# Transposing most of the normalized tokens by DMA in a fused attention and gated-MLP kernel on one Trainium2 core

## The chip, the cores and the metric

The kernel runs on one core of a Trainium2 chip. The core has a matrix engine (PE, TensorE), a vector engine (DVE, VectorE), a scalar engine for activation functions (ACT, ScalarE), a general engine (POOL, GpSimd) and a sync engine (SP) whose queue issues the DMAs here. SBUF is the on-chip working memory of 128 partitions; PSUM holds matmul results in 8 banks. Each engine works through its own instructions in order and waits on semaphores for the others. The metric is the device time of one execution in microseconds (us); lower is better.

## The reference, cut to what matters

```python
x = A_x                              # (1, 2048, 1024), bf16
xn = layernorm(x)                    # no scale, no bias
s = attention(xn)                    # 32 heads of 32: qkv = xn @ wqkv; softmax(q k^T / sqrt(32)) v; @ wo
y = layernorm(xn)
h = gelu(y @ w1 + b1)                # 1024 -> 3584, tanh form
g = silu(h @ w2 + b2)                # 3584 -> 1024
return x + s * g
```

Attention is over all 2048 tokens without a mask. Its 32 x 2048 x 2048 exponentials are the largest amount of elementwise work.

## The kernel before, in words

**Layout.** The 2048 tokens are 16 tiles of 128. Matmuls need the normalized tokens with the model dimension on the partitions, so each tile is normalized token-wise (`xnb`, four buffers used in turn) and transposed into `xnT`, a tensor of 128 partitions x 8 chunks x 2048 tokens. The second layernorm needs no new transpose: `make_y` scales `xnT` by one number per token.

**First stage.** DMAs on SP's queue load the x tiles (line 728), and, between them, the weights for the keys and queries of head group 0 and for the values (lines 739, 744). VectorE takes statistics of each tile (869, 871) and, for a pair of tiles, prepares variance and mean (884, 886). POOL raises the variance to the power -0.5 (888), forms the product with the mean (890) and normalizes each tile into its `xnb` buffer (898); tiles 0 and 1 are normalized by VectorE (879). Then `tr_item` transposes a tile: eight PE transposes against the identity into one PSUM bank (849), and one ScalarE copy of 128x1024 into `xnT` (860; half of tile 1 is copied by VectorE, 858). When both tiles of a pair are there, PE projects their keys (`k_pair_item`, copied out at 814) and, two pairs later in the list, their values (`v_item`, copied out at 786).

**Attention.** Four heads form a head group, and there are eight groups. Work goes by units: group, block of 256 queries, pair of 128-key tiles; 64 units a group, 512 in all. A unit is eight score matmuls on PE (1125), two exponentials on ScalarE of 128x1024 each (1134), and eight PV matmuls (709). The sums of the exponentials over the keys come from VectorE, which adds tiles in three levels (1155, 1160, 1163), and from matmuls with ones; a level that would come late is left out, and PE adds the unsummed tiles instead. `norm` divides (1199 to 1211). Units run in order of their keys, so unit number 7, the last of the first query block, needs the keys of tiles 14 and 15.

**MLP and output.** The MLP runs over chunks of 256 tokens beside the attention, with w1 in a ring of three buffers (936) and w2 in a ring of four (942). Its result goes to DRAM (1041). In the last head group the output projection (`wo`, queue "wo") runs for each query block: four items of eight matmuls, an evacuation that multiplies by the gate (1301), an addition of x (1308, or 1305 on POOL), and a store (1312, 1316). For the last block, matmuls 0 to 6 of an item and matmul 7, which alone needs the last head group, are separate pieces of the order that share a PSUM bank (`host`, `wob`).

**What sets the order.** `_Plan` holds every operation with an assumed duration, its reads and writes and a priority. `run` lays them out on the five engines ahead of time by these assumed durations: scores first on PE, then PV and key sums, then the "dense" queues `pro`, `proj`, `mlp`, `wo`, the last in the order in which items were added. `settle` turns the dependences into semaphore waits, and `emit` writes each engine's instructions in that fixed order. So a changed operation changes the order on every engine, down to the last unit.

Of the kernel before, what the change touches and what calls it, by code (L numbers as in the profile page):

```python
# [40 lines left out]
EVD = ()  # L41
ENGS = ("PE", "ACT", "DVE", "POOL", "SP")
# [7 lines left out]
class _Item:  # L50
    def __init__(self, kind, due=0):
        self.kind = kind
        self.due = due
        self.after = 0
        self.need = []
        self.last = False
        self.host = None
        self.chunks = []
        self.evacs = []
        self.bank = None  # L60
        self.k = 0


class _Plan:
# [3 lines left out]
    def __init__(self):  # L68
# [5 lines left out]
        self.wob = []  # L74
# [39 lines left out]
    def run(self, total_units, dense_slack):  # L114
# [28 lines left out]
        def commit(o, t):  # L143
            e = o.eng
            o.start = t
            if e == "SP":
# [7 lines left out]
                o.fin = state["bw"] + 1900.0  # L154
# [107 lines left out]
        def pe_step(t):  # L262
# [40 lines left out]
            for it in self.wob:  # L303
                if it.k == 0 and it.host.k == len(it.host.chunks) and it.chunks[0].left == 0:
                    cands.append((it.chunks[0].ready, 1.5, it.chunks[0], (it, it.host.bank, None)))
                    break
# [81 lines left out]
            if cls == 1.5:  # L388
                opening[0].bank = opening[1]
            elif opening is not None:  # L390
# [19 lines left out]
            else:  # L410
                it = o.item
                it.k += 1
                if it.k == len(it.chunks):
                    if cls == 1:
                        state["pvopen"] = None
                    elif cls == 1.5:
                        state["done"] += o.occ
# [126 lines left out]
def bass_recurrent_scan__mha_block__mixer_channel_mlp__prompt_kernel(  # L544
# [38 lines left out]
    with ExitStack() as st:  # L583
# [143 lines left out]
        def load_x(t):  # L727
            dma(f"x{t}", lambda e: e.dma_start(xst[t], x2[t * 128:(t + 1) * 128, :]), 262144, [], [XS(t)] + al_x_w(t))

        def al_x_w(t):  # L730
            return []
# [3 lines left out]
        def load_qk(hg, which):  # L735
# [3 lines left out]
            dma(f"wqk{i}", lambda e: e.dma_start(wqk[i], src), 262144 * 3 // 2, [], [("wqk", i)])  # L739
# [13 lines left out]
        for t in range(6, NT):  # L753
            load_x(t)
# [109 lines left out]
        XV = lambda t: ("xst", t)  # L864
        pro_q.append(warm_item())
        for n in range(NPR):
            for t in (2 * n, 2 * n + 1):
                for c in range(2):
# [3 lines left out]
                    150, [("st", t, 0), ("st", t, 1)], [("mv", t)], 1)  # L872
            lo, hi = 2 * n, 2 * n + 2
# [18 lines left out]
            for t in (lo, lo + 1):  # L892
# [5 lines left out]
                pool(lambda e, t=t: e.tensor_scalar(xnb[t % 4], xst[t], lnp[:, t, 1:2], lnp[:, t, 5:6],  # L898
                                                    op0=ALU.mult, op1=ALU.add), 950,
                     [XS(t), ("nb_", n), ("rs", n)], [("xnb", t % 4)], 1)  # L900
            pro_q += [tr_item(lo), tr_item(lo + 1), k_pair_item(n, False)]
# [30 lines left out]
        def load_w1(p):  # L932
# [3 lines left out]
            dma(f"w1{gi}", lambda e: e.dma_start(w1r[gi][:], src), 524288, [], [("w1", gi)])  # L936
# [213 lines left out]
        def ones_four(u, pv):  # L1150
# [15 lines left out]
            def o_fn(e, b):  # L1166
# [13 lines left out]
                return ins  # L1180
            oc = add("PE", lambda e: o_fn(e, pv.bank), Q256, TL,
# [6 lines left out]
            last = HG * 64  # L1188
            for op, more, off in ((add2[0], 2, u < NOPA), (add2[1], 2, u < NOPA or u + 4 >= last),
                                  (add4[0], 1, u < NOPA), (add4[1], 1, u < NOPA or u + 4 >= last),  # L1190
                                  (add8, 1, u < NOPA or u + 4 >= last)):
                if off:
                    plan.skip.append(op)
                    oc.occ += more * Q256
            return oc
# [18 lines left out]
        OTr = xnT  # L1214
        for tq in range(1, 4):
            plan.queues["proj"].append(qk_item(0, 0, tq, wq0, 16 * tq - 12))
            plan.queues["proj"][-1].after = 1000
        for w in range(HG):
# [23 lines left out]
            for qb in range(NQB):  # L1242
# [4 lines left out]
                for kp in range(NKP):  # L1247
# [3 lines left out]
                    if kp % 4 == 3:  # L1251
                        ocs.append(ones_four(g * 8 + kp - 3, pv))
                pv.chunks = [vcs[0:6] + ocs[0:1] + vcs[6:8] + ocs[1:2], vcs + ocs][OLAG]
# [9 lines left out]

                for t2 in range(2):
                    tb = 2 * qb + t2
                    ri = tb % 4
                    if ri < 2:
                        xr = V[:, ri].rearrange("p t n -> p (t n)")[:, 0:1024]
                        gr = V[:, ri].rearrange("p t n -> p (t n)")[:, 1024:2048]
                        rt = [("V", ri, n) for n in range(NPR)]  # L1270
                    elif ri == 2:
                        yf = yT[:].rearrange("p c t -> p (c t)")
                        xr, gr = yf[:, 0:1024], yf[:, 1024:2048]
# [105 lines left out]
```

## Time and profile before

| | us |
|---|---|
| median of three runs (lowest, highest) | 1063.63 (1062.75, 1064.71) |
| the profiled execution | 1063.63 |
| its span in the profile | 1061.6 |
| busy in the span: PE, ScalarE, VectorE, POOL | 1025.0, 1024.8, 972.6, 34.1 |
| granted PE clock, mean | 0.997 |

A group row of the profile names the line of the code, the engine, the operation, the tile written and the tiles read, shapes and count; then the busy time in us and the mean duration of one in ns; then the engine's idle time just before them and what ended most of it. A timeline row gives the start in us, the duration, the engine, line and operation, and in brackets the idle time before it and its releaser. A row of DMA issues ends with the size of one and the median time from issue to landing. Instructions that follow one another on an engine overlap by some tens of ns, so the durations of neighbours can add to slightly more than the stretch they fill. A busy PE is not PE at its peak, since matmuls are pipelined and their ends are modelled.

### The profile page before, as it was taken

To read this page: it belongs to the slowest core of one execution; us is meant where nothing else is said; L and a number is where in the kernel's file an instruction comes from. 1 tells how busy PE (TensorE), PEld (TensorE's weight loads), DVE (VectorE), ACT (ScalarE), POOL (GpSimd) and SP (SyncE) were. 2 spreads that over 40 slices of the span, in tenths; PEclk is the share of its full clock that TensorE was granted. 3 is DMA by queue.
4 is the path that set the end of the run, shared out by engine and by line. 5 is a ranking of instruction groups with operands and counts; after the bars stand their busy time and mean duration, and the time that the engine had idled before them with its cause. 6 is when DMAs were issued, how large, how long until landed. Compare 5 with 4: busy or idle time off the path is not lost.

```text
span 1061.6 us, 32119 instructions
## 1 busy us (share of the span) xinstructions
PE 1025.0 (97%) x14334; PEld 637.7 (60%) x14334; DVE 972.6 (92%) x1506; ACT 1024.8 (97%) x1114; POOL 34.1 (3%) x42
## 2 busy tenths in 40 slices
PE   7898999999999999999999999999999999999998
PEld 5655466646666556656666556656665566665443
DVE  8899999998899999898899989999999899978896
ACT  5899999999999999999999999999999999999994
POOL 5600000000000000000000000000000000000000
PEclk9999999999999999999999999999999999999999
DMA  9334257723276436723365546533566577673442
GB/s 268 91 104 132 58 163 198 212 84 86 76 214 187 114 108 198 202 75 105 104 194 164 144 120 188 166 86 95 143 194 173 160 228 218 195 204 92 140 130 81
DMA packets 285796, 156.49 MB, mean 147 GB/s; under 512 B 23642, under 2 KB 276570, under 8 KB 285658
## 3 DMA queue, kind: packets, MB, share of 16 engines
q1 hardware_dynamic: 285658, 154.44, 50.9%
q8 instruction: 112, 1.84, 0.7%
q14 instruction: 26, 0.21, 0.1%
HBM read 142.35 MB, written 12.06 MB: 145 GB/s over the span
## 4 chain that ended last, share of the span: by engine, by line
PE 48%; ACT 43%; DMA 4%; DVE 3%; POOL 1%; issue 0%; POOLq 0%
ACT P L1134 40%; PE ps L714 32%; PE ps L1125 8%; PE ps L709 8%; DMA w1r<-in_B_w_dram 3%; ACT ut L1000 3%; DVE ut L869 1%; DMA w2r<-in_B_w_dram 1%; POOL gw L898 0%; POOL lnp L912 0%; DMA hT<-in_A_x_dram 0%; DVE xb L985 0%; DVE PA L1155 0%; DVE lnp L884 0%; ACT gw L1036 0%
## 5 line engine op out<-in xcount | busy, mean ns | idle before, releaser
L1134 ACT ACTIVATE P<-ps 128x1024 bf16<-128x1024 f32 x1024 | 960.7, 1189 | 10.2 <-PE ps L1125 9.8
L1155 DVE TENSOR_TENSOR PA<-P 128x2048 bf16<-128x2048 bf16 x251 | 303.9, 1212 | 16.6 <-ACT P L1134 15.4
L714 PE MATMUL ps<-yT,w1r 128*128 128x256 bf16 x1792 | 233.2, 274 | 7.1 <-DMA w1r<-in_B_w_dram 4.4
L714 PE MATMUL ps<-w2r,hT 128*128 128x256 bf16 x1792 | 228.6, 274 | 1.5 <-DVE hT L1003 0.6
L714 PEld LDWEIGHTS ps<-yT,w1r 128*128 128x128 bf16 x1792 | 163.1, 98 | 65.8 <-issue 32.7
L714 PEld LDWEIGHTS ps<-w2r,hT 128*128 128x128 bf16 x1792 | 162.0, 98 | 54.9 <-issue 33.4
L709 PE MATMUL ps<-P,V 128*32 128x256 bf16 x4096 | 146.3, 276 | 1.1 <-ACT P L1134 0.5
L1160 DVE TENSOR_TENSOR PA<-PA 128x1024 bf16<-128x1024 bf16 x202 | 137.8, 689 | 1.7
L714 PE MATMUL ps<-big,qk 128*128 128x512 bf16 (+2 forms) x568 | 130.6, 360 | 2.6 <-DVE V L786 0.8
L714 PE MATMUL ps<-qk,big 128*128 128x256 bf16 (+1 forms) x736 | 124.8, 306 | 0.4 <-DVE V L1301 0.2
L709 PEld LDWEIGHTS ps<-P,V 128*32 128x32 bf16 x4096 | 97.7, 97 | 34.9 <-issue 22.4
L1125 PE MATMUL ps<-qk 32*128 32x256 bf16 x2048 | 102.1, 274 | 9.1 <-ACT P L1134 6.8
L1125 PE MATMUL ps<-QKT 32*128 32x256 bf16 x2048 | 101.7, 273 | 5.0 <-ACT P L1134 4.8
L714 PEld LDWEIGHTS ps<-qk,big 128*128 128x128 bf16 x736 | 65.5, 98 | 39.6 <-issue 15.2
L985 DVE TENSOR_TENSOR xb<-ps,b1T 128x512 bf16<-128x512 f32 x112 | 76.8, 686 | 11.4 <-PE ps L714 10.2
L714 PEld LDWEIGHTS ps<-big,qk 128*128 128x128 bf16 x568 | 47.7, 98 | 54.2 <-issue 15.0
L1003 DVE SCALAR_TENSOR_TENSOR hT<-ut,xb 128x512 bf16<-128x512 f32 x112 | 74.1, 680 | 2.2 <-ACT ut L1000 2.0
L1125 PEld LDWEIGHTS ps<-QKT 32*128 32x128 bf16 x2048 | 30.3, 92 | 72.4 <-ACT P L1134 68.1
L1125 PEld LDWEIGHTS ps<-qk 32*128 32x128 bf16 x2048 | 30.4, 92 | 72.1 <-ACT P L1134 62.4
L998 DVE SCALAR_TENSOR_TENSOR ut<-hT,xb 128x1024 f32<-128x1024 bf16 x56 | 68.2, 1220 | 0.1
L1000 ACT ACTIVATE ut<-ut 128x1024 f32<-128x1024 f32 x56 | 67.3, 1207 | 0.0
L1199 DVE STREAM_TRANSPOSE nt<-ps 128x256 f32<-128x256 f32 x64 | 28.7, 449 | 27.5 <-PE ps L709 27.1
(76 smaller groups left out, 568.5 us busy)
## 6 DMA issues: line engine op xcount, KB each, us to landing
w1r<-in_B_w_dram SPq DMA_DIRECT2D x112, 512.0 KB, 4.6
w2r<-in_B_w_dram SPq DMA_DIRECT2D x128, 448.0 KB, 4.4
qk<-in_A_wqkv_dram SPq DMA_DIRECT2D x16, 256.0 KB, 3.4
g_scratch<-gw SPq DMA_DIRECT2D x32, 128.0 KB, 4.2
o_scratch<-ot SPq DMA_DIRECT2D x56, 64.0 KB, 3.2
big<-o_scratch SPq DMA_DIRECT2D x28, 128.0 KB, 3.7
hT<-in_A_x_dram SPq DMA_DIRECT2D x10, 256.0 KB, 4.5
qk<-in_A_wqkv_dram SPq DMA_DIRECT2D x4, 512.0 KB, 3.8
```

Source lines behind the costliest of these rows:

```text
L709: ins = e.matmul(dst(j), lhsT=lhsT(j), rhs=rhs(j), start=start, stop=stop, tile_position=(0, 32 * j), skip_group_check=True)
L714: return e.matmul(dst, lhsT=lhsT, rhs=rhs, start=start, stop=stop, skip_group_check=True)
L869: dve(lambda e, t=t, c=c: e.bn_stats(stats[:, t, c, :], xst[t][:, c * 512:(c + 1) * 512]), 600, [XS(t)], [("st", t, c)], 1)
L985: dve(lambda e: e.tensor_tensor(xb_t[i2][:, p % 2].rearrange("p (k t) -> p k t", k=2), bank(it.bank).rearrange("p (k t) -> p k t", k=2), b ...
L998: dve(lambda e, r=r: e.scalar_tensor_tensor(ut_t[i2][:, r], h[:, r], 1.0 / GA, xb[:, r], op0=ALU.add, op1=ALU.mult), c_f32(r.stop - r.star ...
L1000: act(lambda e: e.activation(ut_t[i2][:], ut_t[i2][:], ACT.Tanh, scale=GC * GA), c_acts(1024), [("ut", i2, 0), ("ut", i2, 1)], [("ut", i2, ...
L1003: dve(lambda e, r=r: e.scalar_tensor_tensor(h[:, r], ut_t[i2][:, r], 1.0, xb[:, r], op0=ALU.add, op1=ALU.mult), c_f32(r.stop - r.start), [ ...
L1125: ins = e.matmul(bank(b0[j], kk * 256, (kk + 1) * 256), lhsT=QKT[sl][32 * j:32 * j + 32, 1, kb * 128:(kb + 1) * 128], rhs=QKT[sl][32 * j:3 ...
L1134: x = act(lambda e, h=h: e.activation(P[pi][:, 2 * h:2 * h + 2].rearrange("p j k q -> p (j k q)"), ps[:, pr[h] * 1024:(pr[h] + 1) * 1024], ...
L1155: add2.append(dve(lambda e, p0=p0, a0=a0: e.tensor_tensor(PA_all[:, a0:a0 + 2].rearrange("p u j q -> p (u j) q"), P_all[:, p0:p0 + 2, :, 0 ...
L1160: add4.append(dve(lambda e, a0=a0: e.tensor_tensor(PA[a0], PA[a0], PA[a0 + 1], op=ALU.add), c_b16(1024), [("PA", a0 + 1)], [("PA", a0)], P ...
L1199: a = dve(lambda e: e.transpose(nt_t[i][:], bank(pv.bank, 256, 512)), c_ps(256), [], [("nt", i)], 1, pv)
```

## The change

Tiles 0 and 1 are transposed as before. For tiles 2 to 15 the PE transposes and the ScalarE copies are replaced by one DMA each, issued on SP's queue, which reads the `xnb` buffer and writes the tile's columns of `xnT` transposed. A buffer can be overwritten when that DMA has landed. Loads around it are moved: x tile k, for k from 8 on, is not issued before the statistics of tile k - 8 have begun; the third load of key or query weights waits until tile 15 is normalized; the first three w1 loads wait until tiles 9, 11 and 13 are normalized.

The end is changed too. The output projection of the last query block is split in another way: for its four items matmuls 0 to 6 are separate items, added to the queue behind block 5 (`PART`), evacuated to float32 partial sums in SBUF that already contain the gate and x; the last items have one matmul each, an evacuation with the gate and an addition of the partial sum. Their x and gate tiles are in two w1 buffers of their own (numbers 4 and 5). In the last group of four units the key sums' second half is left to PE in two pieces.

```diff
+PART = 5
+TD = 2
+XA = 8
+XB = 8
+XW = 9
...
-                o.fin = state["bw"] + 1900.0
+                o.fin = state["bw"] + (2600.0 if o.sem.startswith("tp") else 1900.0)
...
-        for t in range(6, NT):
+        for t in range(6, XA):
             load_x(t)
...
+                for k in range(XA, NT):
+                    if max(0, k - XB) == t:
+                        load_x(k, [("st", t, 0)])
...
-            pro_q += [tr_item(lo), tr_item(lo + 1), k_pair_item(n, False)]
+            for t in (lo, lo + 1):
+                if t < TD:
+                    pro_q.append(tr_item(t))
+                else:
+
+                    add("SP", lambda e, t=t: e.dma_start_transpose(out=xnT[:, :, t * 128:(t + 1) * 128], in_=xnb[t % 4]),
+                        1500, 0, [("xnb", t % 4)], [("xnT", t, h) for h in range(2)], 0, sem=f"tp{t % 4}", nbytes=360000)
+            pro_q.append(k_pair_item(n, False))
...
-            dma(f"w1{gi}", lambda e: e.dma_start(w1r[gi][:], src), 524288, [], [("w1", gi)])
+            dma(f"w1{gi}", lambda e: e.dma_start(w1r[gi][:], src), 524288, [], [("w1", gi)], 3,
+                [xnop[XW + 2 * p]] if p < 3 else [])
...
+            if hi < HG:
+                dve(lambda e: e.scalar_tensor_tensor(pk, bank(it.bank), 0.5, gr[:, sl], op0=ALU.mult, op1=ALU.mult),
+                    c_ps(512), g, pt, 0, it)
+                dve(lambda e: e.tensor_tensor(pk, pk, xr[:, sl], op=ALU.add), c_f32(512), x + pt, pt, 2.4)
+            else:
+                dve(lambda e: e.scalar_tensor_tensor(gr[:, sl], bank(it.bank), 0.5, gr[:, sl], op0=ALU.mult, op1=ALU.mult),
+                    c_ps(512), g, g, 0, it)
+                if lo == 0:
+                    dve(lambda e: e.tensor_tensor(xr[:, sl], gr[:, sl], xr[:, sl], op=ALU.add), c_b16(512), g + x, x, 1)
+                else:
+                    last = lambda e: e.tensor_tensor(xr[:, sl], gr[:, sl], pk, op=ALU.add)
+                    if t2 == 0:
+                        pool(last, 1100, g + pt, x, 1)
+                    else:
+                        dve(last, c_f32(512), g + pt, x, 1)
...
                 for t2 in range(2):
...
+                    if not lastq:
+                        wo_load(qb, t2)
                     for nh in range(2):
...
+                        wo_item(qb, t2, nh, 7 if lastq else 0, 8)
...
+                if qb == PART:
+
+                    for t2 in range(2):
+                        wo_load(NQB - 1, t2)
+                        for nh in range(2):
+                            wo_item(NQB - 1, t2, nh, 0, 7)
```

## The prediction, made before the changed kernel was run

> **What bounds the kernel now.** I read the busy times first, then stages, then the hand-over between the first stage and the long middle, then the end. In the table of stages each engine's busy time is followed by its number of instructions; the cuts are at the first exponential of the unbroken run (46.0 us) and at the end of the last one (1047.0 us).
>
> ```profile
> PE 1025.0 (97%) x14334; PEld 637.7 (60%) x14334; DVE 972.6 (92%) x1506; ACT 1024.8 (97%) x1114; POOL 34.1 (3%) x42
> ```
> ```profile
> 0.00:46.00 46.00, 36.66 (x398) 26.24 (x399) 39.88 (x96) 29.70 (x33) 31.80 (x40) 1.00 0.68 199
> 46.00:1047.00 1001.00, 977.19 (x13864) 606.38 (x13862) 924.46 (x1395) 995.12 (x1082) 0.00 (x0) 1.00 0.51 146
> 1047.00:1061.60 14.60, 11.15 (x76) 5.07 (x74) 8.25 (x16) 0.00 (x0) 2.31 (x2) 1.00 0.20 72
> ```
> The columns after the length are PE, its weight loads, VectorE, ScalarE and POOL. ScalarE is busy 995.1 of 1001.0 us in the middle: the middle is its exponentials and tanh calls end to end, with 5.9 us of gaps. So the time is three pieces in a row: when the unbroken run starts (46.0), its length (1001), and what follows its last exponential (14.6). In the first stage ScalarE idles 16.3 us, so work taken from it there is worth nothing unless the run starts earlier.
>
> What the removed work costs, from the groups of instructions by shape:
> ```profile
> L1134 ACT ACTIVATE P<-ps 128x1024 bf16<-128x1024 f32 x1024 | 960.7, 1189 | 10.2 <-PE ps L1125 9.8
> L860 ACT ACTIVATE big<-ps 128x1024 bf16<-128x1024 bf16 x15 | 15.1, 1026 | 11.2 <-PE ps L849 11.2
> L849 PE MATMUL ps<-ident,gw 128*128 128x128 bf16 x96 | 7.2, 220 | 3.8 <-DVE gw L879 2.2 <-POOL gw L898 1.6
> ```
> What starts the run, from the timelines of POOL and ScalarE:
> ```profile
> 33.88 1.73 POOL L888 TENSOR_TENSOR lnp<-lnp,mhalf 128x2 f32<-128x2 f32 x1
> 35.69 0.89 POOL L890 TENSOR_TENSOR lnp<-lnp 128x2 f32<-128x2 f32 x1
> 37.20 1.20 POOL L898 TENSOR_SCALAR gw<-w2r,lnp 128x1024 bf16<-128x1024 bf16 x1
> 38.38 1.62 POOL L898 TENSOR_SCALAR yT<-w2r,lnp 128x1024 bf16<-128x1024 bf16 x1
> ```
> ```profile
> 41.83 1.02 ACT L860 ACTIVATE big<-ps 128x1024 bf16<-128x1024 bf16 x1 [0.78 <-PE ps L849]
> 42.75 1.94 ACT L1134 ACTIVATE P<-ps 128x1024 bf16<-128x1024 f32 x2
> 45.98 1.94 ACT L1134 ACTIVATE P<-ps 128x1024 bf16<-128x1024 f32 x2 [1.29 <-PE ps L1125]
> ```
> POOL normalizes one tile after another and ends tile 15 at 40.00. Its transpose, copy, key projection and scores follow, and the first exponential that needs those keys starts at 45.98, which is 5.98 us later. Before it only 14 exponentials (seven units) can run, whatever ScalarE has free. POOL, busy 9.2 and 9.6 of 10 us in 20 to 40 us, and the last tile's path set the start.
>
> The end, from PE's and VectorE's timelines, and the landing times of the DMA issues:
> ```profile
> 1047.17 0.40 PE L709 MATMUL ps<-P,V 128*32 128x256 bf16 x8
> 1048.05 1.25 PE L714 MATMUL ps<-qk,big 128*128 128x512 bf16 x5
> ```
> ```profile
> 1058.19 0.69 DVE L1301 SCALAR_TENSOR_TENSOR w1r<-ps,w1r 128x512 bf16<-128x512 f32 x1 [0.57 <-PE ps L714]
> 1058.92 0.42 DVE L1308 TENSOR_TENSOR w1r<-w1r 128x512 bf16<-128x512 bf16 x1
> ```
> ```profile
> qk<-in_A_wqkv_dram SPq DMA_DIRECT2D x16, 256.0 KB, 3.4
> hT<-in_A_x_dram SPq DMA_DIRECT2D x10, 256.0 KB, 4.5
> w2r<-in_A_x_dram SPq DMA_DIRECT2D x6, 256.0 KB, 6.4
> out_dram<-V SPq DMA_DIRECT2D x8, 256.0 KB, 2.0
> ```
> After the last PV matmuls 46 matmuls of the output projection remain, one per 0.2175 us (five take 1.09). VectorE ends at 1059.34, and 2.26 us later the last store has landed.
>
> **The change, part by part.** The profiled execution took 1063.63 us, the median of the runs; its span is 1061.6, so 2.0 us lie around it.
>
> *Removed in the first stage.* 14 ScalarE copies at 1.026 = 14.4 us, and 14 times 8 PE transposes at some 0.62 = 8.7 us. PE's own share shrinks the backlog in the middle, where PE already waits for ScalarE; ScalarE's share only widens its 16.3 us of idle time. Worth by themselves: 0.
>
> *The transposes' path.* From a normalized tile to its exponential the path was 5.98 us. Now: a DMA of landing time L, then the key projection 1.05, VectorE's copy 0.42, scores to exponential 0.45, and some 0.2 for hand-overs: L + 2.1. The trace has no transposing DMA and none from SBUF to SBUF. Bounds for L are its 256 KB rows: 2.0 (stores) and 6.4 (x tiles behind others). The nearest is the 256 KB load in 256-byte runs, the length that the transposes write, 3.4; since it moves data without turning it, I take 4.5, the next row up. Path 6.6, so +0.6 us (-1.9 to +2.5).
>
> *POOL's new waits.* Each normalized tile sits in one of four buffers. PE freed it at once; now the tile four later waits until the DMA has landed. The built order also puts the power for tiles 8 and 9 ahead of normalizing tiles 6 and 7, so these wait for VectorE's statistics, at some 22.2 us (23.10 before, less a key and a value copy, 1.1, that stand later now, plus a 0.16 copy). Carried through at 1.20 a tile, 0.90 a pair's power and product, with VectorE's statistics at 25.2, 29.4 and 32.4 (3.0 a pair: four at 0.64 and three small steps; 4.2 where a key and a value copy stand between): tiles 6 and 7 end at 25.4 (23.2 before), 11 at 32.7, 13 at 36.0, and, with three small steps (1.6) put in between, tile 15 at 40.0. At L = 4.5 the buffers are free in time; at 6.4 they add 1.2. Before, the last pair lost 1.03 + 0.70 + 0.42 = 2.15 us to stretched steps (1.73, 0.89 and 1.62 against 0.70, 0.19 and 1.20), while VectorE ran its first key sums; those run beside POOL again. I take half: tile 15 at 41.0, +1.0 (-0 to +3.3).
>
> *SP's queue.* 14 transposes are issued ahead of the first w1 and w2 loads. If an issue took 1.84 us, the crowded w1 issue (three in 5.53), 14 would take 25.8, within POOL's 27. x tiles 8 to 15 now wait for statistics of the tile eight before; the last lands at about 22, its statistics come after 29. The weights are issued from some 42 us, three w1 and four w2 at up to 1.84: done by 57, first used near 57: 0, and up to +2 if the cover is gone. The waiting instruction on SP has only those loads behind it.
>
> *The middle.* The same 1010 exponentials and 72 tanh calls run after the start. VectorE gets 3 sums of 1.21, 7 less 1 of 0.69, and four partial results at 0.69 + 0.69: +13.3 us on an engine at 92%. PE loses 8.7 and 1.3 (48 key-sum matmuls at 0.0275). The gaps of 5.9 may shrink or grow: 0 (-4 to +4).
>
> *The end.* The partial sums for the last two token tiles stand in the built order before the previous block's output projection, and are late themselves: 12 of their 28 matmuls stand behind the last PV. After it there are 48 matmuls now, 46 before. First matmul at +0.73 us from the last exponential (+1.06 before; 12 key-sum matmuls fewer), last one through at +11.2, as before. Then it was one evacuation, one add, one store: +14.6. Now the four final matmuls come in a row, so VectorE has a value evacuation until +11.2, four evacuations at 0.64 until +13.8, a 0.42 add, two adds with a float32 operand at 0.65 (0.42 for half the columns, L1211): +15.5. With 2.26 for the store: +17.8. That is +3.2 (+2 to +4).
>
> Sum: 0.6 + 1.0 + 0 + 3.2 = +4.8 us: 1068.4.
>
> A rule of the Trainium skill stands against the change: VectorE: DVE Perf Modes, section "The three transpose paths", gives a 128x128 transpose 390 ns on TensorE and 1309 ns by DMA. This trace shows eight PE transposes in 0.62 us, less than the page says, and no DMA transposes. An estimate by that page, eight blocks one after another, is 10.5 us a tile and 147 us for 14: the kernel would end about 110 us later. DMA: Bandwidth & Descriptors, "Latency and other measured facts", has 261 GB/s for a DMA transpose, by which (an estimate) a tile moves in 1.0 us and my sum holds.
>
> **Rivals.** *Slow transposes.* Above L of some 5 the ring of four buffers paces POOL: each us of L costs about 2.5 us (1.0 on the last path, 1.5 in the ring). L = 8 gives +8.6 at the start and, with the end, 1075; L = 12 about 1085. For: no row excludes it. Against: all 256 KB rows lie under 6.4.
>
> *Nothing to tell.* L near 3 and VectorE's sums clear of POOL: start -1, gaps -1, end +3.2: 1064.8; with the gaps gone 1061.5. For: PE's load falls. Against: the end is plain in the built order.
>
> *Faster.* The removed ScalarE time comes off the start: ScalarE is 9.87 of 10 us busy in 20 to 30 us, and if that, not POOL, paces the first stage, up to 14.4 us go: 1052. It decides once the unbroken run starts before 46.0 - 3.2 - 2.1 = 40.7. Against: tile 15 was normalized only at 40.0, and POOL had gaps of 0.1.
>
> **How the numbers follow.** A change under 0.2% (2.1 us) is about what this kernel's measurement can't tell from none. Forecast (1066 to 1073) 0.56; slow transposes 0.15; nothing to tell 0.15; faster 0.14. Slower is 0.71. All lower bounds at once (-1.9, 0, -4, +2) give 1059.7, all upper ones (+2.5, +3.3, +2, +4, +4) 1079.4. I go from 1061 to 1077, which leaves out some 0.1 of the faster case below and 0.1 of the slow transposes above.
>
> **What would show it.** Right: 14 exponentials before the run, the run's start at 46.5 to 49, transposes landing in 3.5 to 6 us, ScalarE over 99% busy until its last exponential, and 17 to 18 us after it. Wrong: a start before 44 (POOL was held by others), POOL waiting on the transposes for microseconds a tile, ScalarE gaps in the middle beyond 10 us, or an end of 15 us or less.

## The result, and the profile after

The changed kernel took 1072.01 us (median of four runs, 1070.72 to 1073.35) beside 1064.17 for the kernel before: 1.0075 times as long, 95% interval 1.0057 to 1.0094. On another chip it took 1069.66 beside 1063.57, 1.0052 (1.0033 to 1.0071). By these ratios it is slower by 5.5 to 8.0 us; 4.8 had been forecast. Its profiled execution took 1072.81 us with a span of 1071.0.

The stages of the changed kernel, cut at the first exponential of the unbroken run and at the end of the last one, as before (PE, weight loads, VectorE, ScalarE, POOL, clock, DMA share, GB/s):
```profile
0.00:51.67 51.67, 37.58 (x301) 25.55 (x302) 41.74 (x98) 16.57 (x18) 31.97 (x40) 0.87 0.84 190
51.67:1052.82 1001.15, 975.58 (x13810) 603.11 (x13808) 928.06 (x1402) 994.71 (x1082) 0.00 (x0) 1.00 0.53 149
1052.82:1071.00 18.18, 11.38 (x66) 4.95 (x64) 13.64 (x24) 0.00 (x1) 2.28 (x2) 0.91 0.16 58
```
The middle is what it was (1001.15 against 1001.0). The start is 5.7 us later and the end 3.6 us longer. ScalarE lost 13 us of work in the first stage, and its idle time there grew from 16.3 to 35.1 us.

**The start.** POOL's timeline in the changed kernel: the power for tiles 8 and 9, which stands ahead of normalizing tiles 6 and 7; the power for the last pair; and the normalizations of tiles 12, 14 and 15:
```profile
23.62 0.70 POOL L884 TENSOR_TENSOR lnp<-lnp,mhalf 128x2 f32<-128x2 f32 x1 [1.67 <-DVE lnp L882]
...
35.05 0.70 POOL L884 TENSOR_TENSOR lnp<-lnp,mhalf 128x2 f32<-128x2 f32 x1 [1.23 <-DVE lnp L882]
35.73 2.27 POOL L894 TENSOR_SCALAR gw<-w2r,lnp 128x1024 bf16<-128x1024 bf16 x1
...
39.95 2.24 POOL L894 TENSOR_SCALAR gw<-w2r,lnp 128x1024 bf16<-128x1024 bf16 x1
...
43.16 1.19 POOL L894 TENSOR_SCALAR yT<-w2r,lnp 128x1024 bf16<-128x1024 bf16 x1
```
Tile 15 is normalized at 44.35, 4.35 us later than before. POOL waited for VectorE, never for a transpose, and two normalizations took 2.27 and 2.24 us instead of 1.19.

TensorE's timeline in the same kernel, and three windows of 2 us with its granted clock (the third number from the right):
```profile
19.98 1.89 PE L709 MATMUL ps<-qk,big 128*128 128x256 bf16 x8 [3.84 <-DMA big<-gw]
...
28.06 0.61 PE L1129 MATMUL ps<-qk 32*128 32x256 bf16 x8 [3.78 <-DVE qk L807]
28.61 2.10 PE L709 MATMUL ps<-qk,big 128*128 128x256 bf16 x9
30.50 1.91 PE L709 MATMUL ps<-big,qk 128*128 128x256 bf16 x8
```
```profile
10.00:12.00 2.00, 2.00 (x21) 2.00 (x20) 1.60 (x5) 0.12 (x1) 0.00 (x0) 0.50 1.09 338
20.00:22.00 2.00, 2.00 (x10) 1.44 (x11) 2.00 (x5) 0.00 (x0) 1.76 (x3) 0.50 1.15 241
28.00:30.00 2.00, 1.94 (x15) 1.16 (x16) 2.00 (x6) 1.27 (x2) 2.00 (x3) 0.50 0.70 132
```
PE waited 3.84 us for the first transposed tile, and 3.78 us for VectorE's copy of the second pair's keys (L807), which stands behind statistics in VectorE's order. After each wait its clock was granted at half, and eight key matmuls took 1.91 us; in the first stage of the kernel before the clock is 1.00 and they take 1.05 us. The halving at 10 to 12 us comes before the first transposed tile is there.

The last path, from VectorE's and ScalarE's timelines of the changed kernel:
```profile
47.73 0.48 DVE L957 TENSOR_SCALAR qk<-identf,lnp 128x128 f32<-128x128 f32 x2 [2.84 <-POOL lnp L915]
48.13 0.42 DVE L807 CAST qk<-ps 128x256 bf16<-128x256 f32 x1
...
50.46 0.42 DVE L807 CAST qk<-ps 128x256 bf16<-128x256 f32 x1 [0.18 <-PE ps L709]
```
```profile
49.05 1.94 ACT L1138 ACTIVATE P<-ps 128x1024 bf16<-128x1024 f32 x2 [3.55 <-PE ps L1129]
51.67 3.77 ACT L1138 ACTIVATE P<-ps 128x1024 bf16<-128x1024 f32 x4 [0.68 <-PE ps L1129]
```
The two scaled identities for the second layernorm (L957) wait for POOL's last step, and the key copies for tiles 12 to 15 stand behind them. From tile 15 to the start: 7.32 us (5.98 before).

The transposes themselves, from the DMA issues (count, median us from issue to landing):
```profile
big<-gw SPq DMA_TRANSPOSE x10, 3.1
big<-yT SPq DMA_TRANSPOSE x4, 3.2
```

**The end**, from PE's and VectorE's timelines of the changed kernel:
```profile
1062.96 1.24 PE L709 MATMUL ps<-qk 128*128 128x512 bf16 x5
```
```profile
1063.98 2.48 DVE L1279 SCALAR_TENSOR_TENSOR w1r<-ps,w1r 128x512 bf16<-128x512 f32 x4
1066.38 0.93 DVE L1282 TENSOR_TENSOR V<-V 128x512 bf16<-128x512 bf16 x1
1067.23 1.28 DVE L1284 TENSOR_TENSOR w1r<-w1r,hT 128x512 bf16<-128x512 bf16 x2
```
The four one-matmul items come in a row, so VectorE's four evacuations and the additions stand behind the last matmul, as the forecast had it.

### The profile page after: what moved, and what is told of

It is laid out like the page before. It is cut to its first block, busy times and chain, and to the rows that moved or that the text cites. A ratio compares the mean times of both kernels' runs of the same rounds, so it can differ in the third digit from the quotient of the medians.

```text
span 1071.0 us, 31821 instructions
## 1 busy us (share of the span) xinstructions
PE 1024.5 (96%) x14174; PEld 633.6 (59%) x14174; DVE 983.4 (92%) x1523; ACT 1011.3 (94%) x1100; POOL 34.2 (3%) x42
## 4 chain that ended last, share of the span: by engine, by line
ACT 78%; PE 17%; DVE 3%; DMA 1%; POOL 1%; issue 0%; DVEq 0%
ACT P L1138 72%; PE ps L709 11%; ACT ut L1004 4%; PE ps L1129 3%; PE ps L704 3%; DVE ut L862 1%; DMA w1r<-in_B_w_dram 1%; ACT gw L1040 1%; POOL gw L894 0%; POOL lnp L915 0%; DMA hT<-in_A_x_dram 0%; DVE lnp L880 0%; DVE w1r L1279 0%; DVE mv L864 0%; DVE xb L989 0%
## 5 line engine op out<-in xcount | busy, mean ns | idle before, releaser
L1159 DVE TENSOR_TENSOR PA<-P 128x2048 bf16<-128x2048 bf16 x254 | 307.6, 1213 | 21.1 <-ACT P L1138 19.3
L1164 DVE TENSOR_TENSOR PA<-PA 128x1024 bf16<-128x1024 bf16 x209 | 143.0, 691 | 1.2
L709 PE MATMUL ps<-big,qk 128*128 128x512 bf16 (+2 forms) x568 | 134.4, 369 | 2.7 <-DMA big<-gw 1.1
L709 PE MATMUL ps<-qk,big 128*128 128x256 bf16 (+1 forms) x736 | 128.2, 313 | 5.1 <-DMA big<-gw 3.8
L709 PEld LDWEIGHTS ps<-big,qk 128*128 128x128 bf16 x568 | 50.7, 102 | 54.6 <-issue 15.2
```

What stands on the lines that cost most here:

```text
L709: return e.matmul(dst, lhsT=lhsT, rhs=rhs, start=start, stop=stop, skip_group_check=True)
L1159: add2.append(dve(lambda e, p0=p0, a0=a0: e.tensor_tensor(PA_all[:, a0:a0 + 2].rearrange("p u j q -> p (u j) q"), P_all[:, p0:p0 + 2, :, 0 ...
L1164: add4.append(dve(lambda e, a0=a0: e.tensor_tensor(PA[a0], PA[a0], PA[a0 + 1], op=ALU.add), c_b16(1024), [("PA", a0 + 1)], [("PA", a0)], P ...
```

## The experiments

Twelve runs were made in four sets (r_before and r_after are the two kernels again); the runs of a set shared a chip, and each ratio is to the kernel before on that chip (1063.57 to 1064.56 us there). The time is a median. The pieces come from one profiled execution each: when tile 15 is normalized, the start (the first exponential that needs its keys), the path between the two, the middle, and the end piece (us). That execution is not always a typical one: in b_fast (1062.83) and lat32 (1070.34) it lies 2.8 us and more above the median, in best2 (1058.83), p_ord (1064.89) and e_swap (1066.60) 2.1 to 2.6 us below.

| kernel | time | ratio (95%) | tile 15 | path | start | middle | end |
|---|---|---|---|---|---|---|---|
| before | 1064.17 | 1 | 40.00 | 5.98 | 45.98 | 1001.0 | 14.61 |
| changed | 1072.01 | 1.0075 (1.0057, 1.0094) | 44.35 | 7.32 | 51.67 | 1001.2 | 18.18 |
| e_end | 1064.68 | 1.0016 (1.0007, 1.0025) | 40.87 | 5.97 | 46.84 | 998.3 | 17.32 |
| e_front | 1065.60 | 1.0017 (1.0006, 1.0028) | 41.74 | 8.98 | 50.72 | 998.8 | 14.31 |
| e_fill | 1069.40 | 1.0048 (1.0035, 1.0061) | 44.05 | 8.64 | 52.69 | 997.2 | 18.13 |
| e_swap | 1068.71 | 1.0053 (1.0037, 1.0068) | 42.25 | 5.52 | 47.77 | 998.9 | 18.17 |
| r_before | 1064.41 | 1.0006 (0.9994, 1.0017) | 40.08 | 6.59 | 46.67 | 1001.2 | 14.56 |
| r_after | 1069.66 | 1.0052 (1.0033, 1.0071) | 42.27 | 7.32 | 49.59 | 999.9 | 18.14 |
| p_ord | 1067.24 | 1.0031 (1.0018, 1.0044) | 38.32 | 8.52 | 46.84 | 997.8 | 18.19 |
| b_fast | 1059.97 | 0.9970 (0.9956, 0.9983) | 37.50 | 5.78 | 43.28 | 1002.7 | 14.85 |
| lat32 | 1067.52 | 1.0030 (1.0016, 1.0043) | 40.87 | 7.20 | 48.07 | 1001.9 | 18.20 |
| best1 | 1068.77 | 1.0039 (1.0024, 1.0055) | 41.81 | 10.29 | 52.10 | 1000.1 | 15.22 |
| lat32w | 1072.43 | 1.0079 (1.0061, 1.0097) | 41.67 | 8.08 | 49.75 | 1002.0 | 18.19 |
| best2 | 1061.43 | 0.9979 (0.9967, 0.9990) | 38.96 | 6.23 | 45.19 | 997.3 | 14.36 |

**The new end alone (e_end).** All tokens transposed by TensorE, the loads as in the kernel before, the end of the changed kernel (the load edits are left out here):
```diff
-TD = 2
-XA = 8
+TD = 16
+XA = 16
```


> The kernel before with the changed end alone: all sixteen tiles by PE and ScalarE, the old loads, the output projection of the last block split as in the change. Its order is that of before up to the last units. Theory (three pieces in a row: start of the unbroken run, rigid middle, end): the run starts at 46 as before, the last exponential ends at 1047, and 45 matmuls, five evacuations, two adds and a store follow it: end piece some 17.2 us against 14.6, so +2.6 us, 1066.7 against 1064. Rival A (the longer end of the changed kernel is only a consequence of its late start, and the split by itself saves work after the last normalization): end piece 14.6 or less, the same time or faster.

VectorE's four evacuations stand in a row here too:
```profile
1055.47 2.47 DVE L1277 SCALAR_TENSOR_TENSOR w1r<-ps,w1r 128x512 bf16<-128x512 f32 x4
```
The end piece is 17.32, where 17.2 was expected, so rival A falls. The time rose by 1.7 us (0.7 to 2.7 by the interval), less than the 2.7 us of the piece: this execution's middle is 2.7 us shorter than that of the kernel before, although the two orders agree up to the tail (see r_after for what a middle's length goes with).

**The new front alone (e_front).** DMA transposes and moved loads as in the changed kernel, the end of the kernel before put back:
```diff
-PART = 5
...
+            for it in self.wob:
+                if it.k == 0 and it.host.k == len(it.host.chunks) and it.chunks[0].left == 0:
+                    cands.append((it.chunks[0].ready, 1.5, it.chunks[0], (it, it.host.bank, None)))
+                    break
...
-                if qb == PART:
```

> The kernel before with the changed first stage alone: tiles 2 to 15 transposed by DMA, loads moved, the old end. Its order is that of the changed kernel up to the last units. Theory: the unbroken run starts at 51.7 as in the changed kernel, the last exponential ends 5.8 us later than before, the end piece is the old 14.5: +5.7 us, about 1070. Rival B (the freed PE and ScalarE time is made good in the middle, so that the end alone is the loss): the last exponential ends within 2 us of 1047, time within 2 us of before.

The end piece is back at 14.31, but the time rose by 1.8 us only: a miss against 5.7, and inside the 2 us that rival B named for the time. Rival B's reason does not show, since the last exponential ends 2.5 us late, at 1049.5. The start is late, at 50.72 (on the last path the clock was halved once more, 0.50 at 48 to 50 us, and the path is 1.7 us longer than in the changed kernel), and the middle is 2.2 us shorter than that of the kernel before.

**Filler matmuls on TensorE (e_fill).** The changed kernel, with matmuls whose result is overwritten put into its first two waits:
```diff
+                    fill = {v1: (14, dummy, lambda d: d.eng == "SP" and d.sem.startswith("tp")),
+                            plan.s_queue[1]: (16, dummy, lambda d: d.eng == "DVE")}
```


> The changed kernel with 14 filler matmuls of 512 columns put in front of PE's first wait on a transposing DMA and 16 in front of the scores of unit 1, where PE idled 3.8 us each; nothing else is moved. Theory (PE's granted clock falls to half after such idle stretches and the key and value projections behind them, 1.9 instead of 1.05 us each, hold VectorE's statistics of the last tiles and with them POOL): granted clock 1.0 from 16 to 34 us, POOL's wait of 1.2 us for the last pair's statistics gone, tile 15 normalized some 1.2 us earlier than 44.35, start of the run 1 to 1.5 us earlier than 51.7, time about 1070.8. Rival C (the halved clock costs nothing, POOL sets the pace alone): start at 51.7, time as the changed kernel, or later by the fillers.

PE's timeline with the fillers (first row) and the work that waited for the first transposed tile, and a window of the same kernel:
```profile
15.65 3.19 PE L716 MATMUL ps<-ident 128*128 128x512 bf16 x14
22.05 1.59 PE L716 MATMUL ps<-qk,big 128*128 128x256 bf16 x8 [3.20 <-DMA big<-gw]
```
```profile
22.00:24.00 2.00, 1.95 (x11) 1.48 (x12) 2.00 (x8) 0.00 (x0) 0.72 (x2) 0.60 1.20 315
```
The clock was full from 14 to 22 us, but 3.2 us without work were left, and it fell to 0.60 as the first real work came; the second filler then ran until 29.9 us, 2 us past the time at which the keys were there. The start was 1 us later, with the clock halved on the last path as well (0.50 at 50 to 52 us). So the full clock that the theory asked for did not come about, and this run does not tell what the halved clock costs.

**The identities behind the last key copy (e_swap).** The changed kernel with one pair of VectorE's instructions moved:
```diff
+        behind("DVE", dg0, kcopy[NPR - 1])
```


> The changed kernel with VectorE's two scalings of the identity (for the second layernorm, which wait for POOL's power over all 16 tiles) moved behind the copies of the last two key projections; nothing else is moved. Theory (VectorE stands at that wait for 2.8 us while the keys of tiles 12 and 13 are ready at 45.9, and everything behind waits with it): these keys are copied at 46 instead of 48.1, the run starts at about 50.0, set then by the landing of the last transpose at 47.6, and the time falls by 1.7 us to about 1070.3. Rival D (the last transpose's landing sets the start already): the start moves by less than 0.5 us.

VectorE's last key copy and the identities behind it, and ScalarE's start:
```profile
46.56 0.42 DVE L807 CAST qk<-ps 128x256 bf16<-128x256 f32 x1 [0.69 <-PE ps L709]
46.90 0.47 DVE L960 TENSOR_SCALAR qk<-identf,lnp 128x128 f32<-128x128 f32 x2
```
```profile
47.77 7.51 ACT L1143 ACTIVATE P<-ps 128x1024 bf16<-128x1024 f32 x8 [1.23 <-PE ps L1134]
```
The path falls from 7.32 to 5.52 with tile 15 at the same time as in r_after (42.25, 42.27): the wait for the identities was worth 1.8 us at the start, and rival D falls. In the time it cannot be seen: 1.0053 lies among the changed kernel's values.

**Both kernels once more (r_after, r_before).**

> The changed kernel itself again, beside the kernel before on one chip. Theory: the time is start + middle + end piece, and after loses at the start and at the end alone. Ratio 1.005 to 1.009; end piece 18.2; last tile normalized at 42 to 42.5 where the clock stays full at 10 to 12 us and at 44 to 44.5 where it halves there (the start at 49.5 or 51.7). Rival: the middle (1001.2 in the changed kernel, 997 to 999 in the four kernels of the first set) is itself part of the loss: then the middle is again 2 us longer here than in the kernel before on this chip.

> The kernel before itself, for its three pieces on this chip. Theory: start 46.0, end piece 14.6, and the middle as long as that of the changed kernel beside it, within 1.5 us. Rival: its middle is 1001 us here as well while that of the changed kernel is 998 to 999, so that the change gains 2 to 3 us in the middle (PE freed of 8.7 us of transposes), which the first profile of the changed kernel did not show.

POOL's timeline of the changed kernel in this run, and TensorE's clock at 10 to 12 us:
```profile
32.95 0.70 POOL L884 TENSOR_TENSOR lnp<-lnp,mhalf 128x2 f32<-128x2 f32 x1 [0.26 <-DVE lnp L882]
33.63 2.27 POOL L894 TENSOR_SCALAR gw<-w2r,lnp 128x1024 bf16<-128x1024 bf16 x1
...
41.07 1.20 POOL L894 TENSOR_SCALAR yT<-w2r,lnp 128x1024 bf16<-128x1024 bf16 x1
```
```profile
10.00:12.00 2.00, 1.65 (x30) 1.48 (x27) 2.00 (x6) 0.12 (x1) 0.00 (x0) 1.00 0.99 310
```
With a full clock at 10 to 12 us tile 15 is normalized at 42.27 and the run starts at 49.59, 2.08 us earlier than in the first profile, as the theory had it for that case. That early halving is chance: it is in 4 of the 14 profiled executions (changed, e_end, e_fill, best1), with the kernel before's front (e_end, whose start is 0.9 us later than before) as with the new one. Piece by piece, r_after against r_before: start +2.9, middle -1.3, end +3.6, sum +5.2, and the times differ by 5.25. r_before did not start at 46.0 as expected but at 46.67: on its last path the clock was halved, as this row of r_before shows, and the path is 0.6 us longer.
```profile
40.00:42.00 2.00, 1.62 (x8) 1.19 (x9) 0.92 (x2) 1.13 (x2) 1.82 (x4) 0.53 0.29 83
```
Against the first profile of the kernel before, whose last path has a full clock, the start is 3.6 us later.

The middles lie between 997.2 and 1002.7 us, and they go with the clock. Here are the same 6 us with a stretch at half clock (kernel before) and without one (best2):
```profile
96.00:102.00 6.00, 5.31 (x112) 3.80 (x113) 4.28 (x7) 4.58 (x6) 0.00 (x0) 0.72 0.13 38
96.00:102.00 6.00, 5.26 (x130) 4.04 (x131) 5.96 (x11) 6.00 (x8) 0.00 (x0) 1.00 0.31 86
```
A mean of 0.72 over 6 us is 3.4 us at half clock. ScalarE is busy 4.58 us of the 6 with it and 6.00 without. The middles of the traces hold such stretches of 3.4 us, alone or two in a row: three of them in b_fast, lat32 and lat32w (1001.9 to 1002.7), two in each of the two profiles of both kernels (999.9 to 1001.2), at most one in the other seven (997.2 to 1000.1). With two each, the middles of the two kernels differ by 1.3 us or less, so neither a gain nor a loss in the middle is shown, and the rival of r_after falls. What puts a stretch where it is was not tested.

e_end and e_front together cost 0.0033 where the whole change costs 0.0052 and 0.0075. With 0.0009 and 0.0011 either way on the two, this can agree with the second measurement but not with the first; the difference stays open.

**POOL's order of the kernel before, in the changed kernel (p_ord).** With the identities moved as in e_swap:
```diff
+        for n in range(4, NPR):
+            behind("POOL", pw[n], xnop[2 * n - 1])
+        behind("POOL", s2, xnop[NT - 1])
+        behind("DVE", dg0, kcopy[NPR - 1])
```


> The changed kernel with two orders changed and nothing else: POOL takes the power of a pair's variance only after the tiles of the pair before are normalized (as the kernel before does) and the three small steps for the second normalization after tile 15; and VectorE makes the two scaled identities after the last key copy, as in the run with that alone (start 47.77, last tile normalized at 42.25). Theory: the built order of POOL costs the start: tiles 6 and 7 end at 23.3 rather than 25.7, the last pair's power begins at 33.9 at the latest, and tile 15 is normalized at 39 to 39.8 with the stretched steps; start 44.5 to 45.5, about 3 us earlier than with the VectorE order alone, time 4 to 5 us under the changed kernel. Rival: VectorE's statistics, late behind key and value copies that wait for a half-rate PE, pace POOL whatever its order: tile 15 at 41 to 42, start 46.7 to 47.5, and at most 1 us gained over the VectorE order alone.

ScalarE's timeline at the last unit ahead of the start and at the start itself, and the stretch from 28 to 46 us (first number after the length: PE busy):
```profile
44.22 1.94 ACT L1144 ACTIVATE P<-ps 128x1024 bf16<-128x1024 f32 x2 [0.68 <-PE ps L1135]
46.84 3.77 ACT L1144 ACTIVATE P<-ps 128x1024 bf16<-128x1024 f32 x4 [0.68 <-PE ps L1135]
```
```profile
28.00:46.00 18.00, 18.00 (x181) 13.68 (x174) 14.97 (x31) 11.47 (x12) 14.68 (x14) 0.93 0.70 141
```
Tile 15 is ready at 38.32, 3.9 us earlier, and so the order had cost POOL that much. But the start came only 0.9 us earlier than in e_swap: from 28 us on PE was busy without a pause, and from 39 us on a unit came each 2.62 us (keys 1.05, values, scores 0.40). The work that PE had put off in its two waits (3.89 and 3.80 us here), or done at half rate, had become the bound. So POOL's order did cost POOL what the theory said, but the start is where the rival had it, with PE and not VectorE's statistics as the reason. The time is 2.4 us under r_after, about half of what was expected.

**The kernel before, with POOL unburdened (b_fast).** TensorE transposes, old end. POOL's steps for the second layernorm and VectorE's first key sums wait for tile 15, and the identities stand behind the last key copy:
```diff
-             [("rs", n) for n in range(NPR)], [("s2",)], 2)
+             [("rs", n) for n in range(NPR)], [("s2",)], 2, [xnop[NT - 1]])
...
-                    [("P", p0 + i, h) for i in range(2) for h in range(2)], [("PA", a0), ("PA", a0 + 1)], PAPRIO))
+                    [("P", p0 + i, h) for i in range(2) for h in range(2)], [("PA", a0), ("PA", a0 + 1)], PAPRIO,
+                    extra=[xnop[NT - 1]] if u == 0 else ()))
```


> The kernel before (TensorE transposes, old end) with POOL's small steps for the second normalization behind tile 15's normalization, VectorE's first key sums made to wait for that normalization too, and the scaled identities behind the last key copy. Theory: the stretched POOL steps beside VectorE's sums (2.15 us) and the 0.69 step ahead of tile 14 set the start: tile 15 is normalized at 37.2 rather than 40.0, the start is at 43.2 to 44, and the time falls by 2 to 2.8 us. Rival: the stretch comes from VectorE's copies and statistics as well or the path after tile 15 takes up the delayed sums (K7's copy waits): tile 15 at 38 to 39 or a path of 7 to 8 us, and the time within 1 us of before.

POOL's last pair and ScalarE's start in this kernel:
```profile
34.05 0.70 POOL L891 TENSOR_TENSOR lnp<-lnp,mhalf 128x2 f32<-128x2 f32 x1
34.82 0.19 POOL L893 TENSOR_TENSOR lnp<-lnp 128x2 f32<-128x2 f32 x1
35.12 1.20 POOL L901 TENSOR_SCALAR gw<-w2r,lnp 128x1024 bf16<-128x1024 bf16 x1
36.30 1.20 POOL L901 TENSOR_SCALAR yT<-w2r,lnp 128x1024 bf16<-128x1024 bf16 x1
```
```profile
43.28 7.44 ACT L1139 ACTIVATE P<-ps 128x1024 bf16<-128x1024 f32 x8 [0.64 <-PE ps L1130]
```
No step is stretched, tile 15 is ready at 37.50, the run starts at 43.28, and the kernel is faster than both: 0.9970 (0.9956 to 0.9983). Of the 2.7 us, 2.5 come from tile 15 and 0.2 from the path: POOL's chain did set the start of the kernel before.

**One number of the planner (lat32).** The changed kernel; a transpose is assumed to land 3.2 us after its issue:
```diff
-                state["bw"] = max(state["bw"], t) + o.nbytes / 280.0
-                o.fin = state["bw"] + (2600.0 if o.sem.startswith("tp") else 1900.0)
+                if o.sem.startswith("tp"):
+                    o.fin = t + 3200.0
+                else:
+                    state["bw"] = max(state["bw"], t) + o.nbytes / 280.0
+                    o.fin = state["bw"] + 1900.0
```


> The changed kernel with one number of its planner changed: a transposing DMA is taken to land 3.2 us after its issue begins (its median in the trace), rather than 2.6 us after all loads issued before it. Theory: that number put VectorE's copy of the second pair's keys (tiles 2 and 3) at 27.3 us, 7.6 us later than in the kernel before and behind statistics; TensorE waits for it, its clock halves, and it is behind from then on. With the new number that copy comes at 21 to 22.5, TensorE's idle 3.8 us before it is gone, POOL normalizes tiles 6 and 7 ahead of the next pair's power again, tile 15 is normalized at 39.3 to 41, the start is at 45.5 to 47.5 (49.6 in the changed kernel with a full warm-up clock) and the time 2 to 4 us under the changed kernel. Rival: the clock halves anyway because TensorE has nothing to do until the first transposes land (3.9 us up to 19), so the first copies are late whatever their place: start at 48.5 to 50, within 1 us of the changed kernel.

The copy of the second pair's keys, then SP's queue at the end of the first stage, then PE's waits for tiles 12 to 15:
```profile
21.93 0.42 DVE L810 CAST qk<-ps 128x256 bf16<-128x256 f32 x1 [0.37 <-PE ps L712]
```
```profile
33.28 0.64 SPq L949 DMA_DIRECT2D w2r<-in_B_w_dram  x1
33.97 5.21 SPq L905 DMA_TRANSPOSE big<-gw  x2
39.23 0.58 SPq L942 DMA_DIRECT2D w1r<-in_B_w_dram  x1
39.85 2.71 SPq L905 DMA_TRANSPOSE big<-gw  x1
42.61 1.45 SPq L905 DMA_TRANSPOSE big<-yT  x1
```
```profile
41.19 1.05 PE L712 MATMUL ps<-big,qk 128*128 128x256 bf16 x8 [1.84 <-DMA big<-gw]
...
46.06 1.05 PE L712 MATMUL ps<-big,qk 128*128 128x256 bf16 x8 [1.64 <-DMA big<-yT]
```
The copy comes at 21.93, PE's second wait is gone, POOL has its old order by itself, and tile 15 is at 40.87: the theory's first half holds. The time is 2.1 us under r_after, by the ratios 2.3, at the low end of what was expected; the start is at 48.07, not 45.5 to 47.5. In the new order four weight loads stand between the transposes; an issue took up to 3.6 us (median 1.3), and tile 15, normalized at 40.87, was issued at 42.61 and could be used at 46.06.

**Weights behind the transposes (lat32w), and all edits together (best1, best2).** lat32w is lat32 with the first three w1 and four w2 loads waiting for tile 15. best1 is e_front with the planner's new number and the three edits of b_fast; best2 is best1 with the weights behind.
```diff
-                [xnop[XW + 2 * p]] if p < 3 else [])
+                [xnop[NT - 1]] if p < 3 else [])
```


> The run with the planner's landing number of 3.2 us, with one thing more: the first three w1 loads and the first four w2 loads wait for tile 15's normalization, so that SP issues all 14 transposes ahead of them (as the changed kernel does). Theory: with the weights in between, the last transposes took 5.2 us for two issues, 2.7 for one, and landed late (TensorE waited 1.84 and 1.64 us for them); without the weights they land in 2.7 to 3.3 us, the path from tile 15 (40.5 to 41.3) to the start is 5.3 to 6.3 us, the start at 46 to 47.5 and the time 1 to 2 us lower than with the landing number alone. Rival: the transposes are slowed by x loads or by their own number, not by weights: issues stay over 2 us, path 7 or more, no gain.

> The transposes by DMA with the same new landing number, the end of the kernel before (no partial sums for the last two token tiles), POOL's steps for the second normalization behind tile 15, VectorE's first key sums made to wait for tile 15, and the scaled identities behind the last key copy. Theory: the start is set by tile 15 and its path: tile 15 at 37.3 to 38.5, start at 43 to 45, end piece 14.6, middle 997 to 1001, time 1057 to 1061.5, as fast as the kernel before with the last three edits (1060.0) or up to 3 us faster. Rival: TensorE, at half rate until some 24 us, has a backlog at tile 15 that takes the place of POOL (8.5 us from tile 15 to the start, as in the run with POOL's order alone): start at 46 to 47.5 and time 1061.5 to 1064, slower than the kernel before with the three edits; then the transposes by DMA are worth nothing here whatever the order.

> The transposes by DMA with all that the runs before point to: landing number 3.2 us, weights behind the transposes, the end of the kernel before, POOL's steps for the second normalization and VectorE's first key sums behind tile 15, identities behind the last key copy. Theory: tile 15 at 37.5 to 39, path 5.5 to 6.5, start at 43.5 to 45, end piece 14.6 to 15.2, middle 998 to 1002: 1058.5 to 1061.5, level with the kernel before with the last three edits alone (1060.0). Rival: the first transposes leave TensorE idle for 3.9 us and at half rate until some 24 us, and the backlog reaches tile 15: path 7.5 to 9, start 46 to 48, time 1062 to 1065, which the same edits without transposes by DMA beat by 2 us or more.

VectorE's timeline of lat32w on the last path:
```profile
46.29 0.48 DVE L961 TENSOR_SCALAR qk<-identf,lnp 128x128 f32<-128x128 f32 x2 [2.94 <-POOL lnp L918]
46.69 0.68 DVE L1168 TENSOR_TENSOR PA<-PA 128x1024 bf16<-128x1024 bf16 x1
47.29 0.68 DVE L1099 CAST qk<-ps 128x512 bf16<-128x512 f32 x1
47.89 0.41 DVE L810 CAST qk<-ps 128x256 bf16<-128x256 f32 x1
```
In lat32w the longest single issue of a transpose took 1.90 us (3.62 in lat32) and the median landing was 3.2 us (3.7); the last one was issued at 41.70, 0.03 us after its tile was normalized (1.74 us in lat32), and its tile was used at 44.93. So the weights had slowed the transposes. The kernel was slower all the same (1.0079): the order had moved again, and the identities, which wait 2.94 us for POOL, stood ahead of the last key copy once more. That is a miss: another in-order wait took the place of the one removed. best1, without the weights behind, is a miss of its theory and of its rival (1068.77 against 1064 at most): ScalarE stood idle for 6.7 us in one wait for the keys of tiles 12 and 13, which PE projected after waiting 2.64 us for a transpose. best2 has none of these waits, though PE's first wait (3.83 us) and the half clock behind it are still there. It takes 0.9979 (0.9967 to 0.9990), at the upper edge of its theory, about level with b_fast (0.9970), whose three edits it shares. The two ran on different chips and their intervals overlap. Nothing here shows that the DMA transposes add a gain of their own.

## Why the prediction was right or wrong

*Direction and size.* Slower was right. 1068.4 was 3.6 us under the first measurement, inside the range; as a difference, +4.8 stands against +8.0 (6.1 to 10.0) in the first measurement, outside its interval, and +5.5 (3.5 to 7.6) in the second, inside. Of the signs named for being right, the 14 exponentials and ScalarE's 99.4% in the middle came; the start (51.67 and 49.59), the landing time (3.2) and the end piece (18.2) lay outside what was named. None of the signs of being wrong came.

*Removed in the first stage: 0.* ScalarE's 14 copies were worth nothing, as said: it idles more. For PE the step gave no reason why it would keep pace in the first stage. It left out that PE, without its transposes, would wait twice (3.84 and 3.78 us in the first profile) and then run at half rate: in p_ord PE's backlog, and not POOL, set the start. How much of that is the half rate and how much the waits themselves was not separated.

*The transposes' path: L + 2.1, +0.6.* L was taken as 4.5; it is 3.2, median of 14 (2.7 to 5.2), so the estimate of 10.5 us worked out from the Trainium skill, "VectorE: DVE Perf Modes" ("The three transpose paths"), is contradicted. By the step's own formula the path would be 5.3; e_swap, with the identities out of the way, has 5.52. The changed kernel has 7.32. The step failed by leaving out the wait for the scaled identities in VectorE's order, 1.8 us. In the kernel before, VectorE already waited 1.12 us for POOL at these identities, ahead of its last key copy. That the path came out 0.7 us too short and not 2.0 is luck: L was 1.3 us too long.

*POOL's new waits: +1.0.* The working up to tile 11 held within 0.4 us: tiles 6 and 7 at 25.4 (25.79 in r_after), tile 11 at 32.7 (32.68). Then half of 2.15 us was taken for steps stretched beside VectorE's sums. The stretch was 2.5 us (1.07, 0.43 and 1.04 in r_after), so tile 15 came at 42.27 and not 41.0. This term was mis-sized, by 1.3 us. The other 2.1 us of the first profile went with the chance halving at 10 to 12 us. The ring of four buffers never held POOL, as said. That the built order, not the transposes, costs POOL was shown by p_ord (tile 15 at 38.32), and that the planner's landing number made that order by lat32.

*SP's queue: 0.* Right, with the weights behind the transposes as it said. lat32 shows the price without that cover: tile 15 could be used 5.2 us after its normalization instead of 3.2, and PE waited 1.84 and 1.64 us.

*The middle: 0.* +0.15 in the first pair of profiles and -1.3 in the second, within the bounds of 4; with as many half-clock stretches in both kernels no effect is shown.

*The end: +3.2.* +3.6 in both pairs, with VectorE's evacuations and additions where the step put them; e_end shows it alone, +2.7.

*Rivals.* Slow transposes needed a landing time of more than 5 us; it was 3.2. "Nothing to tell" needed a start 1 us earlier; it was 2.9 to 5.7 later. (Its second time does not follow from its terms: with all 5.9 us of gaps gone they give 1059.9, not 1061.5.) "Faster" needed ScalarE to pace the first stage; POOL and then PE did.

## What to carry to other kernels

Moving work off an engine that is waiting buys nothing, and it can cost. TensorE, left with pauses, had its clock lowered in all ten profiles with DMA transposes here. A scheduler that is told a wrong landing time puts instructions behind others in order, where they hold engines that the change never touched. Follow the path instruction by instruction through each queue's order, and look there for a wait on something else that stands ahead of the one needed. Before moving work to another unit, see whether the chain that sets the start can be shortened where it is: three small edits of order did more here than the transposes by DMA. And read the clock of an execution before comparing a piece of it with another's.

## What the runs showed of the hardware that was not expected

- PE's granted clock falls to half after short idle stretches: 0.50 after 3.84 us (changed kernel) and 3.91 us (r_after), 0.60 after 3.20 us (e_fill). The Trainium skill, "TensorE: Matmul & The Clock Gate", section "HAM oscillation — how this bites in real kernels", names gaps above some 3.4 us. Shorter pauses went before a half clock too: 0.50 at 48 to 50 us in e_front after idle stretches of 0.78 and 1.85 us, and 0.53 at 40 to 42 us in r_before after 1.42 and 0.79 us, with work between them.
- From 14 to 34 us the clock was full in all four profiles with PE transposes, and at half for 3.4 us or more in all ten with DMA transposes. A half clock on the last path went with a path longer by 0.6 us in r_before, 1.3 in e_fill and 1.7 in e_front, each against the same order with a full clock there.
- The early halving (between 8 and 12 us) occurs in 4 of 14 executions of kernels with the same work there, and went with a start 2.08 us later between two executions of one kernel. The Trainium skill, "TensorE: Matmul & The Clock Gate", "Part 1: The HAM clock gate (the "warmup" mystery)", says that the window runs freely and the warm-up varies from run to run. Here it is a second fall: the clock is full at 6 to 8 us (1.00 in the changed kernel) before it halves.
- A DMA transpose of 128x1024 bfloat16 from SBUF to SBUF takes 1.27 us to issue (median of the changed kernel; 1.23 to 2.57) and lands after 3.2 us (2.7 to 5.2). With weight loads between them single issues took up to 3.6 us (lat32) and 4.2 us (best1).
- A POOL normalization that begins with a 1.22 us VectorE sum of two SBUF operands takes 2.27 us instead of 1.20, longer by most of that sum. The Trainium skill, "SBUF — State Buffer", section "SBUF: two separate sides", describes a port pair of the two engines that one holds for a whole instruction; with the first sums held back (b_fast) no normalization was longer than 1.20.
